# Expert weights loaded during the last attention slots into tiles that fall free there

## The chip, the cores and the metric

The kernel runs on one core of a Trainium2 chip. The metric is the device time of one execution in microseconds (us). A run of a kernel on one core counts as slow when it is over 1.5% above the fastest of the same kernel; verdicts use the other runs, called fast. Lnnn is a line of the kernel; lines of the changed kernel stand 9 to 30 higher than the same ones of the kernel before. In the views of the profile PE is TensorE (matrix products), DVE VectorE, ACT ScalarE, POOL GpSimd, and SPq the queue of transfers that SyncE issues. The clock is the share of TensorE's full clock that was granted; in the clock records it is either 1.00 or 0.50. An f32 product stands in the traces as two passes.

## The reference, cut to what matters

```python
# 1. DeltaNet attention: q, k, v of (4, 8, 768, 48), a recurrence over 768 tokens
y[:, :, t] = einsum('bhd,bhde->bhe', q[:, :, t], state)
v_old = einsum('bhde,bhd->bhe', state, k_n[:, :, t])
state = state + beta[t] * einsum('bhd,bhe->bhde', k_n[:, :, t], v[:, :, t] - v_old)
# 2. soft MoE: x (3072, 384), phi (384, 32), 8 experts of 4 slots
logits = x @ phi
d = softmax(logits, over tokens);   slot_input = d.T @ x          # 32 x 384
for e in range(8):
    slot_out[e] = relu(slot_input[e] @ w1[e]) @ w2[e]             # w1 384x1024, w2 1024x384
out = softmax(logits, over slots) @ slot_out                      # 3072 x 384
```

Everything is f32. One expert's first or second weights are 1536 KB (1.573 MB), all of them 25.2 MB. The experts need `slot_input`, which is complete only after the last token: whatever of the weights isn't in the core's memory by then is waited for.

## The kernel before

Attention runs in 24 slots, one for each chunk of 32 tokens. Four chunks make a group, and each group's routing (logits, running maximum, exponentials, the product for the experts' slots) is spread over the slots that follow. The last group's routing has nothing to be spread over and runs alone at the end. The parts that matter here:

```python
    for x in range(NCH):                      # 24 slots
        ...
        if 0 <= x + 4 < NCH:
            load_v(x + 4)
        if 8 <= x < 8 + NW1 * NKT:            # NW1 = 1: expert 0's first weights, in thirds
            load_w1((x - 8) // NKT, wpool, NW1, slice((x - 8) % NKT, (x - 8) % NKT + 1))
        ...
    for part in route(NG - 1, ...):           # the last group's routing, alone
        for name in ("head", "act", "mid", "vec", "end"):
            drain(part.get(name, []))
    att.close()                               # attention's memory becomes free

    wp2 = ctx.enter_context(tc.tile_pool(name="wts2", bufs=1, reuse_waits="tile"))
    for e in range(E):
        if e >= NW1:
            load_w1(e, wp2, 4)
        if e % 4 == 3:
            for i in range(e - 3, e + 1):
                load_w2(i, wp2, 6)
    ...                                       # slot inputs sl
    first(0); second(0); first(1); second(1)  # experts 0-3, then 4-7
    sj = wp2.tile([P, Dm], F32, name="sj")
    nc.vector.tensor_copy(sj, pso)            # what both second layers summed
    ...
    for i in range(24):                       # 24 output tiles of 192 KB (cut)
        nc.tensor.matmul(po, lhsT=cT..., rhs=so...)
        ob = wp2.tile([P, Dm], F32, name="ob", tag="ob", bufs=6)
        ...                                   # copy po to ob, on DVE or ACT by turns
        nc.sync.dma_start(out=out[...], in_=ob)
```

All these loads go through one queue, SyncE's, in the order of the built program: in the trace three first weights from 215.8 us, four second weights from 266.6, four first from 268.6, four second from 279.1. A tile in `wp2` lies over attention's dead tiles, and the program has its load wait until the last reader of what it covers is done: the last slots product ends at 266.5 us, and the first second weights go out at 266.61.

## Time and profile before

| | kernel before |
|---|---|
| median of 3 runs | 344.42 us (343.04 to 345.03) |
| span of the profiled run | 341.1 us |
| end of the last slots product (attention's end) | 266.5 us |
| last product of the experts, `sj` begins | 322.3 us |
| from `sj` to the end | 18.8 us |

The first part of the page, each engine's busy time with its share of the span and its instructions:

```profile
PE 276.1 (81%) x6887; PEld 215.8 (63%) x6887; DVE 220.2 (65%) x798; ACT 164.3 (48%) x341; POOL 161.2 (47%) x342
```

An 81% on PE looks like a kernel at its limit. It is an average of two kernels in a row, one short of TensorE and one short of bytes; the prediction takes them apart with the slices, the chain and the queue.

### The profile page before, as it was taken

The page shows a single profiled execution, that of the slowest core. Times are in us where ns is not written, and L with a number is a line of the kernel's source. Part 1 is how long each engine was busy: PE and PEld are TensorE (multiplying, and loading weights), DVE is VectorE, ACT ScalarE, POOL GpSimd, SP SyncE. Part 2 cuts the span into 40 slices and gives each one's busy share as a digit, 9 for nine tenths or more (in the row PEclk, how much of TensorE's full clock was granted, in tenths as well). Part 3 has the DMA queues.
Part 4 walks back from the last instruction along what each step waited for, and adds up shares of the span by engine and source line. Part 5 has one row for each costly group of instructions (what it writes and reads, how often), then busy time and mean ns, then how long its engine had stood idle before and what let it go on. Part 6 is the DMA issues. An engine that isn't in the chain of part 4 may idle for free.

```text
span 341.1 us, 16091 instructions
## 1 busy us (share of the span) xinstructions
PE 276.1 (81%) x6887; PEld 215.8 (63%) x6887; DVE 220.2 (65%) x798; ACT 164.3 (48%) x341; POOL 161.2 (47%) x342
## 2 busy tenths in 40 slices
PE   3885586888889997899989979899995887473884
PEld 3674485777768886788868868788874532020252
DVE  8399989766999897997999999942212210000043
ACT  3463155677758754777568545654752110010042
POOL 8976395648486597429970999932000000000000
PEclk9767659999999999999999995999998999998785
DMA  7855455554554455552012200600062699996078
GB/s 140 158 96 89 79 90 92 84 76 76 84 81 78 74 125 118 91 117 49 16 21 34 40 18 11 209 7 3 4 251 122 238 428 428 431 428 266 0 249 304
DMA packets 79766, 45.22 MB, mean 133 GB/s; under 512 B 73936, under 2 KB 77040, under 8 KB 77776
## 3 DMA queue, kind: packets, MB, share of 16 engines
q1 hardware_dynamic: 77904, 42.98, 45.8%
q0 software_dynamic: 704, 1.03, 1.6%
q8 instruction: 54, 0.88, 1.1%
q10 hardware_dynamic: 1088, 0.20, 0.3%
q14 instruction: 16, 0.13, 0.1%
HBM read 39.47 MB, written 4.72 MB: 130 GB/s over the span
## 4 chain that ended last, share of the span: by engine, by line
PE 46%; DVE 22%; DMA 13%; ACT 10%; issue 4%; SPq 2%; POOL 1%; DVEq 0%; POOLq 0%; ACTq 0%
DMA w2t<-in_moe_w_dram 12%; PE psR L445 7%; PE psS L458 6%; PE pt L596 5%; PE psY L475 4%; PE pt L238 4%; PE pso L891 4%; DVE prM L314 4%; PE psR L431 4%; PE pt L493 4%; ACT S L465 3%; PE pt L209 3%; DVE prE L314 3%; DVE nm L319 3%; DVE tt L319 2%
## 5 line engine op out<-in xcount | busy, mean ns | idle before, releaser
L395 POOL TENSOR_SCALAR V<-V,nT 128x48 f32<-128x48 f32 x192 | 90.8, 497 | 18.9 <-DMA V<-in_v_dram 9.7
L403 POOL TENSOR_SCALAR_AFFINE_SELECT Ab<-GQ 32x256 f32<-32x256 f32 x96 | 48.3, 503 | 12.2 <-PE psY L475 8.0
L465 ACT ACTIVATE S<-psS 48x768 f32<-48x768 f32 x46 | 37.1, 806 | 23.7 <-PE psS L458 23.4
L445 PE MATMUL psR<-R,Tb 64*64 64x48 f32 x768 | 29.7, 227 | 9.4 <-DVE R L438 6.7
L238 PE MATMUL pt<-KQ 48*32 48x64 f32 (+1 forms) x1792 | 25.7, 231 | 12.0 <-ACT KQ L225 6.8
L445 PEld LDWEIGHTS psR<-R,Tb 64*64 64x64 f32 x768 | 26.6, 141 | 13.2 <-issue 5.8
L238 PEld LDWEIGHTS pt<-KQ 48*32 48x32 f32 x1792 | 20.7, 115 | 18.3 <-ACT KQ L225 8.5
L319 DVE TENSOR_TENSOR nm<-nm,prM 128x16 f32<-128x16 f32 (+7 forms) x96 | 30.3, 316 | 0.0
L314 DVE TENSOR_TENSOR prM<-tt,lb 128x16 f32<-128x16 f32 (+7 forms) x96 | 30.1, 314 | 0.0
L475 PE MATMUL psY<-U,Ab 64*64 64x48 f32 x768 | 28.1, 224 | 0.1
L242 ACT ACTIVATE GQ<-pt 128x256 f32<-128x256 f32 (+1 forms) x56 | 16.7, 351 | 22.1 <-PE pt L238 21.5
L438 DVE TENSOR_TENSOR R<-V,psR 128x384 f32<-128x384 f32 x24 | 13.2, 550 | 21.1 <-PE psR L431 15.2
L475 PEld LDWEIGHTS psY<-U,Ab 64*64 64x64 f32 x768 | 25.1, 138 | 2.7 <-issue 0.7
L319 DVE TENSOR_TENSOR tt<-tt,prE 128x30 f32<-128x30 f32 (+7 forms) x90 | 25.6, 285 | 0.0
L458 PE MATMUL psS<-U,K 32*112 32x96 f32 x736 | 25.5, 278 | 0.0
L314 DVE TENSOR_TENSOR prE<-tt,lb 128x30 f32<-128x30 f32 (+7 forms) x90 | 25.3, 281 | 0.2 <-DVE nm L319 0.2
L448 ACT ACTIVATE U<-psR 128x384 f32<-128x384 f32 x24 | 11.8, 492 | 27.7 <-PE psR L445 22.7
L408 ACT ACTIVATE Tb<-TT,own 128x256 f32<-128x256 f32 x48 | 21.7, 504 | 6.1 <-DVE TT L386 6.1
L458 PEld LDWEIGHTS psS<-U,K 32*112 32x112 f32 x736 | 21.6, 183 | 4.1 <-issue 1.7
L431 PE MATMUL psR<-S,KQ 128*32 128x96 f32 x768 | 22.4, 258 | 1.2 <-ACT S L465 0.7
L431 PE MATMUL psY<-S,KQ 128*32 128x96 f32 x768 | 22.1, 256 | 1.2 <-issue 1.2
L891 PE MATMUL pso<-w2t,hT 128*32 128x384 f32 x128 | 16.0, 585 | 8.6 <-DMA w2t<-in_moe_w_dram 8.1
(143 smaller groups left out, 538.6 us busy)
## 6 DMA issues: line engine op xcount, KB each, us to landing
w2t<-in_moe_w_dram SPq DMA_DIRECT2D x8, 1536.0 KB, 18.8
w1t<-in_moe_w_dram SPq DMA_DIRECT2D x7, 1536.0 KB, 14.5
Q<-in_q_dram SPq DMA_DIRECT2D x96, 48.0 KB, 2.8
out_dram<-ob SPq DMA_DIRECT2D x24, 192.0 KB, 2.4
K<-in_k_dram SPq DMA_DIRECT2D x88, 48.0 KB, 2.6
V<-in_v_dram SPq DMA_DIRECT2D x80, 48.0 KB, 2.7
w1t<-in_moe_w_dram SPq DMA_DIRECT2D x3, 512.0 KB, 4.3
V<-in_v_dram POOLq DMA_DIRECT2D x16, 48.0 KB, 3.2
```

Of the source, the lines that this page charges most:

```text
L238: nc.tensor.matmul(pg[g][rh, b], lhsT=kq[r, b, 0, rh], rhs=kq[r, b, a0:a1, rh], start=True, stop=True, skip_group_check=True)
L314: nc.vector.tensor_tensor(pr, a.broadcast_to([P] + shape), b.broadcast_to([P] + shape), op=ALU.mult)
L319: nc.vector.tensor_tensor(dst, dst, pr, op=op)
L395: nc.gpsimd.tensor_scalar(Vt[cc][:, u], Vt[cc][:, u], nT[n][:, c * U + u:c * U + u + 1], None, op0=ALU.mult)
L403: nc.gpsimd.affine_select(out=Ab[cc % NT][r, :, h % 2, :].rearrange("p (b g) t -> p b g t", g=G), in_=GQ[n][r, c, :, :, 1, :], compare_op= ...
L408: nc.scalar.activation(Tb[cc % 2][:, :, x, :], TT[n][:, c * U:(c + 1) * U, :], ACT.Identity, scale=own[:, x:x + 1])
L431: nc.tensor.matmul(dst[hs[h], b].rearrange("p g d -> p (g d)"), lhsT=kq[:, b, a, hs[h]], rhs=old[:, h, b, :], start=(b == 0), stop=False, ...
L445: nc.tensor.matmul(pw[half[y], u], lhsT=T[y][:, u], rhs=st["R"][half[y], u], start=(u == 0), stop=True, skip_group_check=True)
L458: nc.tensor.matmul(psS[0:DP + D, h, b * GD:(b + 1) * GD], lhsT=K[hs[h], b * G:(b + 1) * G].rearrange("p g d -> p (g d)")[:, 0:DP + D], rhs ...
L465: nc.scalar.activation(new[r, :, :, g * D:(g + 1) * D], psS[r, :, 0:B * GD].rearrange("p h (b g e) -> p h b g e", b=B, g=G)[:, :, :, g], A ...
L475: nc.tensor.matmul(qs[half[y], b, g], lhsT=at[y][:, u], rhs=st["U"][half[y], u], start=False, stop=True, skip_group_check=True)
L891: nc.tensor.matmul(pso[C * j:C * j + C], lhsT=hT[q][:, t, C * j:C * j + C], rhs=w2t[4 * q + j][:, t, :], start=(q == 0 and t == 0), stop=( ...
```

## The change

Intent: issue first weights while the queue is nearly idle. Tiles that attention no longer needs in its last nine slots, such as a chunk's transposed keys and queries, are moved into a pool that outlives attention, and take 21 pieces of first weights (512 KB each). Second weights go into what is dead then and into tiles that the first layers set free.

```diff
+    lp = ctx.enter_context(tc.tile_pool(name="long", bufs=1))
...
-            KQ[cc] = wk.tile([P, B, 2, P], F32, name="KQ", tag="KQ", bufs=LEAD + 1)
+            KQ[cc] = lp.tile([P, B, 2, P], F32, name="KQ", tag="KQ", bufs=LEAD + 1)
...                      (GQ, tt, lb, TT and the Q tiles move to lp likewise)
+    free = {15: "GQ", 16: "KQ tt Q0 Q1", 17: "KQ", 18: "KQ", 19: "KQ TT GQ", 20: "KQ tt lb",
+            21: "KQ", 22: "KQ", 23: "KQ TT GQ"}
     for x in range(NCH):
...
+        preload(free.get(x, ""))     # one first-weight piece into each tile (two into a GQ)
...
-    for e in range(E):
-        if e >= NW1:
-            load_w1(e, wp2, 4)
-        if e % 4 == 3:
-            for i in range(e - 3, e + 1):
-                load_w2(i, wp2, 6)
+    for e in range(5):
+        load_w2(e, range(NFC), wp2.tile([P, NFC * Dm], F32, name="w2t", tag="w2t", bufs=5))
...
     first(0)
+    load_w2(5, range(NFC), wpool.tile([P, NFC * Dm], F32, name="w2t", tag="w0", bufs=1))
+    for t in range(0, NFC, 2):
+        load_w2(6, range(t, t + 2), room("KQ"))
+    load_w2(7, range(0, 5), room("GQ"))
+    load_w2(7, range(5, 7), room("KQ"))
+    load_w2(7, range(7, 8), room("tt"))
+    first(1)
     second(0)
-    first(1)
     second(1)
...
-            ob = wp2.tile([P, Dm], F32, name="ob", tag="ob", bufs=6)
+            ob = wp2.tile([P, Dm], F32, name="ob", tag="ob", bufs=10)
```

More of the change, by code (lines that the diff above doesn't have):

```diff
@@ L77 @@
     Ks = [io.tile([P, U, DP], F32, name=f"K{i}", bufs=1) for i in range(NK)]
-    Qs = [io.tile([P, U, DP], F32, name=f"Q{i}", bufs=1) for i in range(NQ)]
+    Qp = [lp.tile([P, 2, U, DP], F32, name=f"Q{i}", bufs=1) for i in range(NQ // 2)]
+    Qs = [Qp[i // 2][:, i % 2] for i in range(NQ)]
     Vt = {}
@@ L175, with room, load_w1, load_w2 @@
         nc.vector.memset(t, 0.0)
-    NW1 = 1
-    w1t, w2t = {}, {}
-    def load_w1(e, pool, bufs, parts=None):
-        if e not in w1t:
-            w1t[e] = pool.tile([P, NKT, F], F32, name="w1t", tag="w1t", bufs=bufs)
-        src = moe_w1[e].rearrange("(p k) f -> p k f", k=NKT)
-        if parts is None:
-            nc.sync.dma_start(out=w1t[e], in_=src)
-        else:
-            nc.sync.dma_start(out=w1t[e][:, parts], in_=src[:, parts])
-    def load_w2(e, pool, bufs):
-        w2t[e] = pool.tile([P, NFC, Dm], F32, name="w2t", tag="w2t", bufs=bufs)
-        nc.sync.dma_start(out=w2t[e], in_=moe_w2[e].rearrange("(p t) d -> p t d", t=NFC))
+    w1s = [[None] * NKT for _ in range(E)]
+    w2s = [[None] * NFC for _ in range(E)]
+    LONG = dict(KQ=([P, F], LEAD + 1), GQ=([P, 2 * F], 3), tt=([P, F], 2), lb=([P, F], 1),
+                TT=([P, F], 2))
+    def room(tag):
+        if tag in LONG:
+            shape, bufs = LONG[tag]
+            return lp.tile(shape, F32, name="w" + tag, tag=tag, bufs=bufs)
+        return Qp[int(tag[1])].rearrange("p a u d -> p (a u d)")
+    cells = [(e, k) for e in range(1, E) for k in range(NKT)]
+    def load_w1(e, ks, t):
+        nc.sync.dma_start(out=t[:, 0:len(ks) * F].rearrange("p (k f) -> p k f", f=F),
+                          in_=moe_w1[e].rearrange("(p k) f -> p k f", k=NKT)[:, ks[0]:ks[-1] + 1])
+        for i, k in enumerate(ks):
+            w1s[e][k] = t[:, i * F:(i + 1) * F]
+    def load_w2(e, ts, t):
+        nc.sync.dma_start(out=t[:, 0:len(ts) * Dm].rearrange("p (t d) -> p t d", d=Dm),
+                          in_=moe_w2[e].rearrange("(p t) d -> p t d", t=NFC)[:, ts[0]:ts[-1] + 1])
+        for i, j in enumerate(ts):
+            w2s[e][j] = t[:, i * Dm:(i + 1) * Dm]
+    def preload(tags):
+        for tag in tags.split():
+            t = room(tag)
+            for i in range(2 if tag == "GQ" else 1):
+                e, k = cells.pop(0)
+                load_w1(e, [k], t[:, i * F:(i + 1) * F])
     KQ, GQ, TT, nT = {}, {}, {}, {}
@@ L230, in products @@
             if n not in GQ:
-                GQ[n] = wk.tile([P, GC, B, G, 2, C], F32, name="GQ", tag="GQ", bufs=3)
+                GQ[n] = lp.tile([P, GC, B, G, 2, C], F32, name="GQ", tag="GQ", bufs=3)
             pg = [pt([P, B, na, C]) for _ in range(G)]
@@ L259, in unit @@
         def unit():
-            tt = st["tt"] = wk.tile([P, size], F32, name="tt", tag="tt", bufs=2)
+            tt = st["tt"] = lp.tile([P, size], F32, name="tt", tag="tt", bufs=2)
             nc.gpsimd.memset(tt, 0.0)
@@ L269, in spread @@
         def spread():
-            lb = st["lb"] = wk.tile([P, size], F32, name="lb", tag="lb", bufs=1)
+            lb = st["lb"] = lp.tile([P, size], F32, name="lb", tag="lb", bufs=1)
             nc.vector.transpose(
@@ L383, in back @@
             if n not in TT:
-                TT[n] = wk.tile([P, C, C], F32, name="TT", tag="TT")
+                TT[n] = lp.tile([P, C, C], F32, name="TT", tag="TT", bufs=2)
             r = slice(half * HC, (half + 1) * HC)
@@ L752 @@
             load_v(x + 4)
-        if 8 <= x < 8 + NW1 * NKT:
-            load_w1((x - 8) // NKT, wpool, NW1, slice((x - 8) % NKT, (x - 8) % NKT + 1))
+        if 8 <= x < 8 + NKT:
+            if x == 8:
+                w0 = wpool.tile([P, NKT * F], F32, name="w0", tag="w0", bufs=1)
+            load_w1(0, [x - 8], w0[:, (x - 8) * F:(x - 7) * F])
+        preload(free.get(x, ""))
         follow = plan(n + 2) if c == GC - 1 and n + 2 < NG else None
@@ L812 @@
     pp = ctx.enter_context(tc.tile_pool(name="pp", bufs=1, space=PSUM, reuse_waits="tile"))
-    for e in range(E):
-        if e >= NW1:
-            load_w1(e, wp2, 4)
-        if e % 4 == 3:
-            for i in range(e - 3, e + 1):
-                load_w2(i, wp2, 6)
+    assert not cells
+    for e in range(5):
+        load_w2(e, range(NFC), wp2.tile([P, NFC * Dm], F32, name="w2t", tag="w2t", bufs=5))
     def bank(tag, shape):
@@ L867, in product @@
                     nc.tensor.matmul(ph[C * j:C * j + C], lhsT=sl[:, k, :],
-                                     rhs=w1t[4 * q + j][:, k, f * HF:(f + 1) * HF],
+                                     rhs=w1s[4 * q + j][k][:, f * HF:(f + 1) * HF],
                                      start=(k == 0), stop=(k == NKT - 1), skip_group_check=True)
@@ L891, in second @@
                 nc.tensor.matmul(pso[C * j:C * j + C], lhsT=hT[q][:, t, C * j:C * j + C],
-                                 rhs=w2t[4 * q + j][:, t, :],
+                                 rhs=w2s[4 * q + j][t],
                                  start=(q == 0 and t == 0), stop=(q == 1 and t == NFC - 1),
```

## The prediction

> **What bounds the kernel now.** The first view is the page's table of 40 slices, each 341.1 / 40 = 8.5 us long.
>
> ```profile
> PE   3885586888889997899989979899995887473884
> DVE  8399989766999897997999999942212210000043
> PEclk9767659999999999999999995999998999998785
> GB/s 140 158 96 89 79 90 92 84 76 76 84 81 78 74 125 118 91 117 49 16 21 34 40 18 11 209 7 3 4 251 122 238 428 428 431 428 266 0 249 304
> ```
>
> Two kernels in a row. Counting slices from 0, up to slice 30 (about 265 us) the attention half runs, in 24 slots (chunks of 32 tokens): PE is full, DVE to slice 26, and from slice 18 to 28 the DMA engines move almost nothing. From slice 32 to 35 it is the other way round: the queue runs flat at 428 to 431 GB/s, DVE is at 0 or 1 and PE has holes. Then come the outputs. The second view is the chain of work that ended last, from 262 us on.
>
> ```profile
> 262.32 4.22 PE pt L596 x64
> ...
> 266.56 0.02 SPq L193
> ...
> 267.94 15.93 DMA w2t<-in_moe_w_dram
> ...
> 283.91 4.78 PE pso L891 x55
> ...
> 289.08 25.01 DMA w2t<-in_moe_w_dram
> ...
> 314.14 8.09 PE pso L891 x58
> ...
> 322.26 0.57 DVE sj L907
> ```
>
> L596 is the last product of attention, L193 the issue of second weights, L891 the second layer. Of the 55.7 us between 266.56 and 322.26, 15.93 + 25.01 = 40.9 are waits for weights. Why they come so late is in the queue's own order of time:
>
> ```profile
> 215.84 34.48 SPq L187 DMA_DIRECT2D w1t<-in_moe_w_dram  x3
> 266.61 1.94 SPq L193 DMA_DIRECT2D w2t<-in_moe_w_dram  x4
> 268.60 10.41 SPq L187 DMA_DIRECT2D w1t<-in_moe_w_dram  x4
> 279.06 10.41 SPq L193 DMA_DIRECT2D w2t<-in_moe_w_dram  x4
> ```
>
> Three first-weight tiles went out before attention ended. The other twelve (4 + 4 + 4, 1536 KB = 1.573 MB each, 18.9 MB) start at 266.6 and end at 314.1: 47.5 us. By rate: 18.9 MB / 430 GB/s = 43.9 us, and the last landing is 2.6 us past the pure stream (four tiles issued at 266.6 are all there at 283.9: 17.3 us against 4 x 3.66 = 14.6), so 46.5; 1 us stays unexplained. This stretch is bound by bytes, and only by the bytes that wait for attention's memory. The third view is the table by stretch, whose columns are stretch, length, then busy time of PE, PEld, DVE, ACT, POOL with counts, clock, DMA share and GB/s:
>
> ```profile
> 288.00:296.00 8.00, 4.34 (x19) 0.91 (x12) 0.00 (x0) 0.00 (x0) 0.00 (x0) 1.00 1.01 429
> 304.00:312.00 8.00, 3.68 (x17) 1.25 (x14) 1.44 (x2) 0.59 (x1) 0.00 (x0) 1.00 1.01 432
> 312.00:320.00 8.00, 5.86 (x40) 1.91 (x44) 0.00 (x0) 0.00 (x0) 0.00 (x0) 0.57 0.04 13
> 328.00:336.00 8.00, 7.53 (x24) 5.17 (x24) 3.91 (x8) 3.85 (x8) 0.00 (x0) 0.62 1.03 367
> ```
>
> DMA is full to 312. Then PE, which had starved, gets its last weights at 314.14 and runs at a clock of 0.57: its 58 products take 8.09 us where the same work at full clock took 4.78 (x55). The last line is the output stage: 367 GB/s of writes.
>
> [...] The loads here run at 428 to 432[...]. [...] here a first 1.573 MB tile lands after 6.2 us at the least, 2.5 us over its 3.66. [...] matmuls after the gap that ended at 314.14 (2.85 us, with only 2 matmuls in the 6.1 us before it) pace at 0.16 us, before and later at 0.08; single gaps of 1.7 to 2.8 us between 280 and 300 left the clock at 1.00.
>
> **The change part by part.** I built both kernels and compared instruction order and tile addresses. On POOL, DVE and ACT the order is the same; on PE it differs only after attention. Instruction counts don't change, nor do bytes (25.2 MB of weights). What moves is the time at which 21 pieces of first weights and some second weights start.
>
> 1. First weights, experts 1 to 7: 21 pieces of 512 KB (11.0 MB) go out in slots 15 to 23, each into a tile whose last reader is in an earlier slot. In the trace before, slots 15 to 23 are 183 to 252 us, nearly free of DMA; 11.0 MB at 430 is 25.6 us of 69. The last three pieces wait for the last chunk's weights (ACT at 249.6) and land by about 256. Nothing of it reaches the path: first layers start at 269.8 (as before).
>
> 2. Second weights: experts 0 to 4 lie in the pool opened after attention, over its dead tiles. In the built program, expert 0's tile lies over K tiles that are dead long before, and goes out right behind the last first weights (about 250, landing about 260), as does a quarter of expert 6. Expert 1's tile lies over the last `dr`, read until 266.54, and the queue is in order: so 1 to 4 start at 266.6, exactly like the first four of before, landed at 283.9. Behind them 2.75 tiles remain (5, three quarters of 6, 7). They wait for the first layer of experts 0 to 3, which ended at 277.7, while the queue is still busy to about 282; so there is no hole. 2.75 x 3.66 = 10.1 us: the last byte lands at 283.9 + 10.1 = 294.0, and expert 7's first five eighths 3/8 x 3.66 = 1.4 us earlier, at 292.6. Path before: 314.1. Saved on the stream: 20 us.
>
> 3. PE: first layer of 0 to 3 to 277.7, as before. In the built order the second half-layer follows with the turns woven in: 8 matmuls, 8 transposes (1.13 us), 40 matmuls at 0.1076 us (four in 0.43 us in the timeline, f32 products are two passes each): 278.7 + 1.2 + 4.3 = 284.2; mask, turns and copies of before took 304.9 to 307.2, i.e. 2.3, so 286.6. Second layer of 0 to 3: 64 passes x 0.081 = 5.2, four of them already done: 291.5. Second layer of 4 to 7 needs expert 7's first piece from its fourth product on: it stops at about 291.9 and goes on at 292.6, with 58 passes x 0.081 = 4.7: 297.3. [...] this costs 4.7 where before it cost 8.1. PE and DMA end almost level here: with all weights in place PE alone would end at 296.7.
>
> 4. The end: from the last product to the end of the span 341.1 - 322.3 = 18.8 us, mostly writes. The output tiles go from 6 to 10. In the chain the first outputs are spaced 0.50 us, by issue; later ones 0.54 us, by waiting for a free tile. At most 24 x 0.04 = 1 us is to be had; the DMA share of 1.03 says that the engines are nearly full anyway, so I take 0.4.
>
> Sum: last product 322.3 to 297.3, -25.0; outputs -0.4: span 341.1 to 315.7. The timed median is 344.42, so 344.4 - 25.4 = 319.0.
>
> **The rivals.** (a) *Nothing gained, as the bytes are the same.* If DMA bound the whole kernel, moving loads would not help. The GB/s row speaks against it: eleven slices with 3 to 49 GB/s apart from one. Time would stay at 344. (b) *The early loads slow attention.* They share the in-order queue with V, and in slots 16 to 19 a V load stands behind up to four pieces (2.1 MB, 4.9 us). V is loaded four slots ahead and first touched two slots later, some 16 us of slack at 8 us a slot; and the built waits name readers of the slot before. In the trace before, the 1.5 MB load at 215.8 and those at 250 went by without slots becoming longer. I grant 0 to 3 us. (c) *A tile frees later than meant and the queue stalls*, so that experts 4 to 7 land after 278 and PE waits for first weights. The margin is about 20 us; a full loss of step 1 would give some 15 us back (time about 334). (d) *PE as the new bound, cold.* [...] 64 passes at 0.16 cost 5 us more: 324. (e) *Smaller pieces move slower* (3 KB per partition and less in 2.36 MB)[...].
>
> **Range and chances.** Steps 2 and 3 rest on measured paces, and two independent limits meet within a microsecond, so a miss of one of them shows at once: (b), (d) and (e) all lengthen. On the short side, attention itself varies with the clock (the three runs of before spread 2 us), and outputs may gain the full 1 us. 315.5 to 323.5 holds it 8 times in 10. Faster by over 2% means under 337.5; only (a) or a full (c) with more on top prevents it: 0.97, 0.02, 0.01.
>
> **What would show it.** In the changed profile: DMA filled to some 150 to 200 GB/s in slices of 183 to 252 us; the last slots product as before at about 266.5 (if later than 269, rival b); no PE wait on first weights (else c); one run of about 430 GB/s from 267 to 294; a clock of 1.00 through the second layer (else d); the chain going from slots over transfers of `w2t` or the borrowed tiles to the last `pso` at about 297; from there 18.4 us to the end. The prediction is wrong if second weights other than experts 0 and part of 6 start before 266, or if the stream has a hole at 277 to 283 because the queue reaches expert 5's issue late.

## The result

The changed kernel took 326.0 us, median of 4 fast runs (322.73 to 327.15), beside 344.73 us for the kernel before in the same rounds. The ratio is 0.9445, with a 95% interval of 0.9365 to 0.9525: faster. (Ratios are the mean time of one kernel's fast runs over that of the other's of the same rounds, so not quite the ratio of the medians.) The time lies outside the predicted range of 315.5 to 323.5, on the long side. The profiled run is the longest of its four (span 325.4 us), whereas the profiled run of before lay 1.6 us under its median; this matters below.

The slices of the changed kernel, 8.1 us each:

```profile
PE   2896747888979999799998998796999958996890
PEclk9958559999999999679999999787899977999995
GB/s 132 164 100 90 69 91 94 70 88 89 81 79 82 78 83 129 93 82 130 50 13 26 144 175 220 91 87 259 202 69 66 221 218 112 432 422 341 4 308 273
```

From slice 22 (179 us) the DMA engines now move 66 to 259 GB/s beside attention, where in most slices they moved next to nothing before; the flat stretch at 422 to 432 GB/s has shrunk from four slices and a half to not quite three (34 to 36), and PE is full in the first two of them. In the clock row, slices 16, 17, 25 to 28, 32 and 33 show 6 to 8. The kernel before had only slices 24 and 30 under 9 between the start-up and its last layer.

The chain that ended last:

```profile
264.71 1.71 PE pt L597 x8
...
267.75 4.94 PE pt L615 x64
...
284.06 16.41 DMA wGQ<-in_moe_w_dram
300.52 5.36 PE pso L914 x58
305.90 0.57 DVE sj L937
```

It has the predicted shape: last slots product, first layers, one transfer, the 58 last passes. But the slots product ends at 272.7 and not at 266.5, expert 7's first piece (`wGQ`) lands at 300.5 and not at 292.6, and the 58 passes take 5.36 us and not 4.7. The queue, from the first early load on:

```profile
182.93 0.82 SPq L196 DMA_DIRECT2D wGQ<-in_moe_w_dram  x2
...
255.19 0.86 SPq L196 DMA_DIRECT2D wGQ<-in_moe_w_dram  x2
256.10 26.45 SPq L202 DMA_DIRECT2D w2t<-in_moe_w_dram  x6
...
284.06 0.43 SPq L202 DMA_DIRECT2D wGQ<-in_moe_w_dram  x1
```

All 21 pieces are issued by 256. Then the issues of expert 0 to 5 second weights stretch over 26.45 us: expert 0's goes out at once, at 256.1, expert 1's waits in front of everything behind it until attention's memory is free, and goes out at 272.7. So much had been read out of the built program. The stretch by stretch table (columns as in the prediction) around the end of the stream:

```profile
280.00:288.00 8.00, 7.97 (x74) 2.81 (x66) 1.44 (x2) 1.96 (x3) 0.00 (x0) 1.00 1.02 435
288.00:296.00 8.00, 7.66 (x84) 3.31 (x80) 1.44 (x2) 0.58 (x1) 0.00 (x0) 1.00 1.00 413
296.00:304.00 8.00, 5.01 (x58) 1.81 (x54) 0.00 (x0) 0.00 (x0) 0.00 (x0) 1.00 0.48 193
```

PE is full beside a full DMA, then has 3 us of holes in the last row, at a clock of 1.00. The view of waits names them: engine, line, what it waited for, us in total, times, longest.

```profile
PE pso L914 <- DMA wGQ<-in_moe_w_dram: 3.0, 1, 3.0
```

Laid beside the prediction's sum, for the profiled spans:

| stretch | predicted | measured | difference |
|---|---|---|---|
| start to the end of the last slots product | 266.54 | 272.69 | +6.15 |
| from there to expert 7's first piece landed | 26.1 | 27.83 | +1.7 |
| 58 passes of the second layer, to `sj` | 4.7 | 5.4 | +0.7 |
| `sj` to the end | 18.4 | 19.5 | +1.1 |
| span | 315.7 | 325.4 | +9.7 |

The medians miss by only 7.0 us: the profiled run of before lay 1.55 us under the median from which the prediction took its 25.4, and the profiled run of the change lies 1.15 us above its own.

### The profile page after: what moved, and what is told of

It is laid out like the page before. It is cut to its first block, busy times and chain, and to the rows that moved or that the text cites.

```text
span 325.4 us, 16112 instructions
## 1 busy us (share of the span) xinstructions
PE 269.7 (83%) x6887; PEld 217.0 (67%) x6887; DVE 219.7 (68%) x798; ACT 163.9 (50%) x341; POOL 160.5 (49%) x342
## 3 DMA queue, kind: packets, MB, share of 16 engines
q0 software_dynamic: 704, 1.03, 1.7%
## 4 chain that ended last, share of the span: by engine, by line
PE 50%; DVE 27%; DMA 8%; ACT 6%; issue 4%; SPq 3%; DVEq 0%; ACTq 0%
PE psR L464 6%; PE pt L615 6%; PE psS L477 6%; DMA wGQ<-in_moe_w_dram 5%; DVE prM L333 5%; PE psY L494 5%; PE psR L450 4%; PE pt L257 4%; PE pt L228 4%; DVE prE L333 4%; DVE nm L338 4%; PE pt L512 3%; DVE tt L338 3%; ACT S L484 2%; PE psY L450 2%
## 5 line engine op out<-in xcount | busy, mean ns | idle before, releaser
L422 POOL TENSOR_SCALAR_AFFINE_SELECT Ab<-GQ 32x256 f32<-32x256 f32 x96 | 48.0, 500 | 16.9 <-PE psY L494 12.7
L464 PE MATMUL psR<-R,Tb 64*64 64x48 f32 x768 | 29.0, 224 | 9.4 <-DVE R L457 6.4
L464 PEld LDWEIGHTS psR<-R,Tb 64*64 64x64 f32 x768 | 26.0, 139 | 13.0 <-issue 7.0
L257 PEld LDWEIGHTS pt<-KQ 48*32 48x32 f32 x1792 | 20.8, 116 | 18.7 <-ACT KQ L244 10.6
L338 DVE TENSOR_TENSOR nm<-nm,prM 128x16 f32<-128x16 f32 (+7 forms) x96 | 30.2, 314 | 0.0
L494 PE MATMUL psY<-U,Ab 64*64 64x48 f32 x768 | 29.7, 231 | 0.1
L494 PEld LDWEIGHTS psY<-U,Ab 64*64 64x64 f32 x768 | 26.6, 145 | 2.7 <-issue 0.8
L477 PE MATMUL psS<-U,K 32*112 32x96 f32 x736 | 26.4, 285 | 0.0
L477 PEld LDWEIGHTS psS<-U,K 32*112 32x112 f32 x736 | 22.4, 189 | 4.1 <-issue 1.7
L450 PE MATMUL psR<-S,KQ 128*32 128x96 f32 x768 | 23.2, 264 | 1.6 <-issue 0.9
L615 PE MATMUL pt<-Y,dr 64*64 64x97 f32 x384 | 21.6, 272 | 1.8 <-ACT dr L606 1.4
```

What stands on the lines that cost most here:

```text
L257: nc.tensor.matmul(pg[g][rh, b], lhsT=kq[r, b, 0, rh], rhs=kq[r, b, a0:a1, rh], start=True, stop=True, skip_group_check=True)
L338: nc.vector.tensor_tensor(dst, dst, pr, op=op)
L422: nc.gpsimd.affine_select(out=Ab[cc % NT][r, :, h % 2, :].rearrange("p (b g) t -> p b g t", g=G), in_=GQ[n][r, c, :, :, 1, :], compare_op= ...
L450: nc.tensor.matmul(dst[hs[h], b].rearrange("p g d -> p (g d)"), lhsT=kq[:, b, a, hs[h]], rhs=old[:, h, b, :], start=(b == 0), stop=False, ...
L464: nc.tensor.matmul(pw[half[y], u], lhsT=T[y][:, u], rhs=st["R"][half[y], u], start=(u == 0), stop=True, skip_group_check=True)
L477: nc.tensor.matmul(psS[0:DP + D, h, b * GD:(b + 1) * GD], lhsT=K[hs[h], b * G:(b + 1) * G].rearrange("p g d -> p (g d)")[:, 0:DP + D], rhs ...
```

## The experiments

My theory after the result: the bytes were taken off the path as predicted, and the largest miss, the later end of attention, is a matter of TensorE's clock at chance moments, not of the loads. The rival is the prediction's rival (b): the early loads lengthen the slots. Eleven runs were made, in three sets, each set on another chip and beside the kernel before (medians 344.41, 345.13 and 344.69 us); two of them repeat a kernel.

### Attention alone, with and without the early loads

In four kernels the expert layers are cut out, and the output stage takes a constant row. Their outputs are wrong, which doesn't matter for the times. Two come from the kernel before, two from the changed one (these with 6 output tiles, as before), each with and without loads.

```diff
 # short_after_none: the changed layout, no early loads
-    free = {15: "GQ", 16: "KQ tt Q0 Q1", ...}
+    free = {}
 # short_after_loads: all 21 pieces, expert 0's w2, a quarter of expert 6's; GpSimd reads one
 # column of each piece at the very end, so that none is dropped
+    nc.gpsimd.tensor_copy(junk[:, ...], w1s[e][k][:, 0:1])
 # all four: layers cut
-    first(0) ... second(1)
-    nc.vector.tensor_scalar(so, ps4, rd, None, op0=ALU.mult)
+    nc.vector.tensor_scalar(so, sacc[:, 0:1].broadcast_to([P, Dm]), rd, None, op0=ALU.mult)
```

> The kernel before with the expert layers cut out (the output stage multiplies by a constant row instead, so the result is wrong on purpose) and no expert weights but expert 0's first ones. It times attention plus the output stage alone, on the old layout, with nothing loaded late. Attention ended at 266.5 us in the profile before; about 3 us of set-up and 15.2 us of outputs follow, so about 286 to 288 us timed. This is the base of a two by two comparison: layout (old, new) and weight loads during attention (none, as in each kernel).

> The same with the three first-weight loads that the kernel before issues during the end of attention (1536 KB each). Theory 'chance' (attention's length differs between executions by spells of half clock, and loads do not matter): within 1.5 us of short_before_none. Theory 'loads slow attention': longer by an amount in proportion to 4.7 MB of 13, 1 to 2 us.

> The changed kernel cut in the same way, no weights loaded in slots 15 to 23. It tells the layout (tiles at other addresses) from the loads. Theories 'chance' and 'loads' both say within 1.5 us of short_before_none; a theory 'layout' (shared Q tiles, other addresses) says 2 us or more longer.

> The changed kernel cut in the same way, with all 21 first-weight pieces in slots 15 to 23 and expert 0's second weights behind them, as the changed kernel has them (each piece is touched once at the end by GpSimd so that its tile stays taken). Theory 'chance': within 1.5 us of short_after_none, and the profile shows half-clock spells at other places than the others, before slot 15 too. Theory 'loads slow attention', which is my rival b: 3 to 5 us longer than short_after_none, with the delay arising in slots 15 to 23.

| kernel | median us, fast runs | range | fast runs of 6 |
|---|---|---|---|
| short_before_none | 288.84 | 287.83 to 291.62 | 6 |
| short_before_loads (three late loads, as before) | 288.93 | 288.22 to 290.62 | 5 |
| short_after_none | 289.53 | 288.04 to 291.95 | 5 |
| short_after_loads | 290.95 | 289.43 to 292.95 | 5 |

The differences, 0.1 and 1.4 us for the loads and 0.7 and 2.0 us for the layout, are no larger than the scatter of each kernel over its own fast runs, some 2.4 to 3.9 us. As times, these runs leave room for either effect up to about 3 us. The two profiles of the changed layout say more, as both happened to have their clock spells in the same places. (Both were taken in runs that count as slow, 295.28 and 296.12 us, so they are compared only with each other.) TensorE's timeline in the last chunk, first without and then with the loads (start, us, engine, line, operation; a bracket gives idle time before it and what ended it):

```profile
256.70 1.14 PE L464 MATMUL psR<-R,Tb 64*64 64x48 f32 x32 [0.69 <-DVE sel L854]
...
261.50 1.55 PE L615 MATMUL pt<-Y,dr 64*64 64x97 f32 x32
```

```profile
256.72 1.14 PE L464 MATMUL psR<-R,Tb 64*64 64x48 f32 x32 [0.69 <-DVE sel L863]
...
262.15 0.38 PE L512 MATMUL pt<-ident,Y 128*96 128x128 f32 x2 [0.77 <-issue]
262.46 1.55 PE L615 MATMUL pt<-Y,dr 64*64 64x97 f32 x32
```

After 24 slots and 11 MB of loads beside them, the same product starts at 256.70 and 256.72 us. In this pair the loads did nothing to the slots. Only behind it does the kernel with loads lose 1 us, most of it in one pause of 0.77 us in which the profile shows nothing that TensorE waits for ("issue"). Whether its next instructions came late because of the stream is not shown, and nothing below rests on it. The same test over all thirteen profiles stands further down.

### Everything as in the change, but the first weights issued after attention

```diff
-        preload(free.get(x, ""))                     # in the slots
+    for x in sorted(free):                           # after attention
+        preload(free[x])
 # and in preload, a tiny GpSimd copy of attention's last result into each tile holds it back:
+            nc.gpsimd.tensor_copy(t[:, 0:1], sacc[:, 0:1])
```

> The changed kernel with the early loading undone: the 21 first-weight pieces go into the same tiles, but each tile gets a few numbers copied from attention's last result first, so that no piece can start before attention ends (the copies are overwritten by the load, the result stays right). The stream after attention is then 11.0 MB longer, 25.6 us at 430 GB/s. Stream: 23.2 MB, 54 us + 2.6 us after attention's end, then about 5 us of products and 19.5 us of outputs. Expected about 350 us (347 to 353), that is slower than the kernel before, which loads a quarter of that early; if the stream were not what the change shortens, it would stay near 326 us.

Correct, 352.03 us (349.96 to 354.9, 4 fast runs), ratio 1.0248 (1.0184 to 1.0312): slower than the kernel before, though whether by 2% stays unclear, as the interval includes it. Its chain:

```profile
270.60 8.32 DMA wKQ<-in_moe_w_dram
...
304.77 16.99 DMA wGQ<-in_moe_w_dram
321.81 7.05 PE pso L915 x58
```

The path after attention consists of transfers again, 62.0 us from the end of the slots product (266.9) to `sj`, against 33.2 in the changed kernel. The early start of the first weights is worth 29 us there and 26 us of the median. All of the change's gain comes from it: without it the kernel is 7 us slower than before, which had at least started three of these tiles (4.7 MB) ahead of attention's end. Its last layer also shows rival (d): after a pause of 4.2 us on TensorE the 58 passes take 7.05 us, not 5.36.

### The old order of the layers, and the old number of output tiles

```diff
 # layers_old
-    first(1)
     second(0)
+    first(1)
     second(1)
 # ob6
-            ob = wp2.tile([P, Dm], F32, name="ob", tag="ob", bufs=10)
+            ob = wp2.tile([P, Dm], F32, name="ob", tag="ob", bufs=6)
```

> The changed kernel with the layers in the old order: first and second layer of experts 0 to 3, then of 4 to 7. It tells what the second half of the change is worth. With it TensorE waits for second weights of experts 0 to 3 (the last landed 14 us after attention's end in the changed kernel, while their first layer is done 13 us after), then does the first layer of 4 to 7 (5 us) and its turns (2.3 us) while the stream runs; all is ready about 30 us after attention's end, the stream's last pieces at 28. Expected: same within 1.5 us; if the order matters, 2 to 4 us slower.

> The changed kernel with 6 output tiles instead of 10, as before. From the last second-layer product to the end the changed kernel took 19.5 us, before 18.8. Theory 'more tiles help the outputs' (my prediction, 0.4 us): 0.4 us longer. Theory 'writes are bound by the transfers, the tiles do not matter, or more in flight does harm': same within 0.5 us, or 0.6 us shorter, that is a stretch of 18.8 us in the profile.

layers_old is correct with 326.47 us (322.16 to 329.14), three of its six runs slow (the fast ones alone: 322.88); ratio of the fast ones 0.9382 (0.9329 to 0.9435). From the end of attention to `sj` it takes 32.5 us, where the changed kernel took 33.2 and, on its second run below, 32.5. The order of the layers is worth nothing that these few fast runs can show: either way the last layer stands waiting for expert 7 (3.0 us in the change, 2.0 here).

ob6 is correct with 325.66 us (323.45 to 327.22), ratio 0.9447 (0.9401 to 0.9494), so the time of the change itself (from attention's end to `sj` it took 34.8 us in its profile, so this stretch too differs by 1 to 2 us between profiles of the same program). Waits of DVE for an output tile, first with ten tiles (the change) and then with six, and the issue of the 24 outputs in the kernel before, the change and ob6:

```profile
DVE ob L951 <- DMA out_dram<-ob: 3.1, 6, 0.5
```

```profile
DVE ob L951 <- DMA out_dram<-ob: 5.6, 9, 1.5
```

```profile
325.95 12.14 SPq L924 DMA_DIRECT2D out_dram<-ob  x24
```

```profile
309.60 12.15 SPq L954 DMA_DIRECT2D out_dram<-ob  x24
```

```profile
309.09 12.16 SPq L954 DMA_DIRECT2D out_dram<-ob  x24
```

With more tiles DVE waits less, and the queue issues the 24 outputs in the same 12.15 us. What sets this pace is the transfers. In the packet records of all three runs an output has landed every 0.54 us from the first to the last (192 KB in 0.536 us are 367 GB/s), while the issues begin at a spacing of 0.50 us and fall back to 0.54 after about fourteen. Four more tiles gain nothing here. What remains of step 4 is that the span ends 3.65 us after the last issue in the change and in ob6, and 3.0 in the kernel before. This 0.65 us lies behind the outputs: from the last output packet to the end of the span it is 1.97 us in the change and in ob6, and 1.32 in the kernel before. In that time SyncE goes through ten semaphore instructions instead of five.

### A tile of its own for each of the five second weights

A tag names a set of buffers that tiles take by turns. In the built change, the five `w2t` buffers of one tag were laid out so that expert 1's tile covers what the last slots product reads. Expert 1's load stands second of them in the queue and goes out at 272.7 us, as attention ends. Experts 2 to 7 (but for a quarter of 6, issued at 253.9) follow it from 273.1 on, although much of what they cover is long dead. With tags of their own the tiles come in ascending order: experts 0 to 2 lie over tiles that die earlier, and only experts 3 and 4 have to wait.

```diff
-        load_w2(e, range(NFC), wp2.tile([P, NFC * Dm], F32, name="w2t", tag="w2t", bufs=5))
+        load_w2(e, range(NFC), wp2.tile([P, NFC * Dm], F32, name=f"w2t{e}", tag=f"w2t{e}", bufs=1))
```

> The changed kernel, but the five second-weight tiles of experts 0 to 4 get tags of their own, which puts them in ascending order over the dead attention tiles: experts 0 and 1 over K tiles, 2 over K, V and S, and only 3 and 4 over the tiles that are read until attention's end. So three tiles instead of one go out before attention ends. In the changed kernel TensorE stood 3.0 us waiting for expert 7's first piece. Theory 'the stream is still the last limit by 3 us, TensorE just behind': the wait goes, and the time falls by 2.5 to 3 us, to about 323. Theory 'my prediction's balance was right and the rest is attention': the wait would be under 1 us and nothing is gained.

Correct, 321.39 us (319.43 to 325.73, two of six runs slow; the fast ones alone 320.87), ratio 0.9311 (0.9267 to 0.9356). To rule out luck, it ran again beside the change itself:

> The changed kernel once more, unchanged, to see how far its attention half differs from run to run. If the attention half ends at a chance time set by half-clock spells (my theory), its profile may show the end of the last slots product anywhere from about 266 to 275 us (first profile: 272.7), and fast runs of 322 to 328 us. If the early loads lengthen it (rival), it is again at 272 or later. From there to the last layer's result 33 us, as before (33.2), whatever attention did.

> The version with a tag for each second-weight tile once more, beside the changed kernel on the same chip. If the gain of about 4.5 us is the stall before expert 7 and the late start of the stream, it repeats: 321 us, 3.5 to 5 us below the changed kernel of this call, and 29.4 us from the end of the last slots product to the last layer's result. If it was a lucky attention half, the two kernels lie within 1 us here.

after_again: 324.53 us (323.78 to 326.43, 6 fast runs), ratio 0.9452 (0.9404 to 0.95). own_again: 321.45 us (319.1 to 323.72, 6 fast runs), ratio 0.9356 (0.9295 to 0.9416). The gain repeats, as 3.1 us of the medians. Attention in after_again's profile ended at 270.2 and the rest took 32.5 us, both as the theory of chance has it (the rival wanted 272 or later). The gain of own_again was no lucky attention either: in these two profiles attention ends *later* with tags of their own (272.1 against 270.2). The gain is behind it, in own_again's chain:

```profile
278.01 5.28 PE ph L890 x46
...
291.00 10.49 PE pso L914 x124
```

No transfer is left in it. Both second layers run as one row of 124 products to 301.5, which is 29.4 us after attention's end, to the tenth what own_tags' first profile gave (268.7 to 298.2). The prediction had worked out that "with all weights in place PE alone would end at 296.7", which is 30.2 us after 266.54. That number was nearly right; the stream's was not, and the change was bound by the stream.

### TensorE kept busy through the last routing

The clock's part could be tested by itself. On top of own_tags, fifteen useless products of 128 by 128 go into the pauses of the last group's routing, into a tile of PSUM that is dead by then.

```diff
 # in route(), for the last group alone; t is lT or dT, which are in place at that point
+                    nc.tensor.matmul(psS[:, i % 4, 0:P], lhsT=ident, rhs=t, start=True, stop=True,
+                                     skip_group_check=True)
 # 3 before over_rows' turn, 1 behind by_tokens', 5 behind spread_max's, 6 behind repeat's
```

> As own_again, with 18 products of no use (128 by 128, into a dead tile) put into the pauses of the last routing, where TensorE rests, to keep its clock. Results stay right. If the half-clock spell at the end of attention (262 to 266 us at 0.50 in the earlier profile) comes from these pauses, the clock there is 1.00 (or at least 0.9), the four products before the slots take 1.1 instead of 2.1 us and the slots product 4.2 instead of 4.5, and the median is 1 to 2 us below own_again's. If spells come whatever TensorE does [...], the clock is as low as before and the time is the same or up to 1 us longer, for the added products.

The expectation says 18 products; there are 15, each of two passes in the trace. Correct, 318.33 us (315.86 to 321.26, one of six runs slow; the fast ones alone 317.80), ratio 0.9251 (0.9189 to 0.9312), 3.1 us below own_again in the median, where 1 to 2 were expected. The end of the routing in own_again, in TensorE's timeline and in a row of the table by stretch:

```profile
264.38 2.08 PE L597 MATMUL pt<-ident,dT 128*128 128x128 f32 x8 [1.09 <-ACT dT L587]
267.81 4.28 PE L615 MATMUL pt<-Y,dr 64*64 64x97 f32 x64 [1.36 <-ACT dr L606]
```

```profile
266.00:270.00 4.00, 2.64 (x31) 2.35 (x31) 0.00 (x0) 1.26 (x2) 0.00 (x0) 0.50 1.00 427
```

And the same two views of warm_end, where L608 and L627 are these two lines and L524 is the added product:

```profile
261.73 1.16 PE L608 MATMUL pt<-ident,dT 128*128 128x128 f32 x8
262.72 1.50 PE L524 MATMUL psS<-dT,ident 128*128 128x128 f32 x12
264.24 2.88 PE L627 MATMUL pt<-Y,dr 64*64 64x97 f32 x64
```

```profile
262.00:266.00 4.00, 3.98 (x62) 3.79 (x63) 0.20 (x2) 1.26 (x2) 0.00 (x0) 1.00 1.01 430
```

The same eight passes of L597 (L608) take 1.16 instead of 2.08 us, the same 64 of the slots product 2.88 instead of 4.28, at a clock of 1.00 instead of 0.50; for the slots product 4.2 had been expected. In own_again the clock falls at 263.9 us, after a pause of 0.81 us and in the middle of one of 1.09. From the end of the last logits to the end of the slots product it is 8.7 us instead of 10.5. That much, 1.8 us, comes from the clock in the routing's pauses: no other of the thirteen profiles has this stretch under 9.5 us. The means of the fast runs differ by 3.6 us (321.42 and 317.80), with an error of about 0.9 from the scatter of the runs; the rest may be scatter, and isn't explained here. From attention's end to `sj` it takes 29.4 us once more (267.1 to 296.5).

### All profiles side by side

Each run left one profile, so attention's end can be compared over thirteen. "Cold" is the time lost to a low clock, worked out from the table by stretch in steps of 4 us: the sum of 2 x (1 - clock) x 4, that is the us spent at half clock. The start-up is left out: there it is 10 to 31 us, and yet the second chunk begins its `psR` product within 57.2 to 58.8 us in all thirteen. The early loads begin at about 183 us. (The kernel before and short_before_loads have three loads from 216 us on; short_after_none and short_after_loads are slow runs.)

| profile | early loads | cold, 60 to 180 us | cold, 180 us to the last logits | last logits end | from there to the slots product's end | attention's end |
|---|---|---|---|---|---|---|
| before | no | 0.0 | 10.2 | 257.0 | 9.5 | 266.5 |
| late | no | 0.0 | 10.2 | 256.1 | 10.7 | 266.9 |
| short_before_loads | no | 0.0 | 10.2 | 258.1 | 10.7 | 268.8 |
| short_before_none | no | 0.0 | 13.6 | 259.4 | 11.7 | 271.1 |
| short_after_none | no | 10.2 | 17.0 | 264.1 | 10.7 | 274.8 |
| layers_old | yes | 0.0 | 6.9 | 258.4 | 10.7 | 269.1 |
| own_tags | yes | 0.0 | 13.7 | 258.0 | 10.7 | 268.7 |
| ob6 | yes | 0.0 | 13.6 | 259.0 | 11.7 | 270.6 |
| warm_end | yes | 3.4 | 10.2 | 258.4 | 8.7 | 267.1 |
| after_again | yes | 10.2 | 3.4 | 259.5 | 10.7 | 270.2 |
| own_again | yes | 12.7 | 6.9 | 261.6 | 10.5 | 272.1 |
| after | yes | 10.2 | 13.7 | 261.9 | 10.7 | 272.7 |
| short_after_loads | yes | 10.2 | 17.1 | 265.0 | 10.4 | 275.4 |

Add the two cold columns and the last logits follow them to within 1 to 2 us, loads or no loads: 256 to 258.4 at 7 to 10 us, 258 to 259.5 at 13 to 14, 262 at 20 to 24, 264 to 265 at 27. At 13.6 to 13.7 the kernels with loads are at 258.0 to 259.5 and the one without at 259.4. Nor do the loads make more cold time: beside them it is 3.4 to 17.1 us from 180 on (mean 10.7), without them 10.2 to 17.0 (mean 12.2). And the profile of before is the shortest of all thirteen, with a shorter tail than any but warm_end, which was made to be warm.

The slots themselves say the same. From chunk 15's `psR` product (L445, L464) to chunk 23's, which is the time of the early loads, it is 64.0 us in the kernel before and 66.9 in the change; over the five profiles without early loads 64.0 to 67.5 (mean 66.1), over the eight with them 64.5 to 67.5 (mean 66.6). The kernel before is again the shortest.

Nor do the cold spells come out of nothing. In TensorE's timelines each of the 25 spells at half clock that begin between 60 and 250 us has, in the 3.4 us before it, at least part of a pause of 1.4 to 2.9 us (in one case two pauses, of 1.15 and 0.64). The 3.4 us are the length of the shortest of these spells (one from 94.3 us in warm_end, one from 215.0 in after_again); the others last 6.8 to 6.9 or 10.2. The pauses stand before a `psR` product, which mostly waits for DVE's tile `R` (before three of the four spells in the profiles of before and the change; before the fourth, at 132.0 us in the change, the profile shows nothing that is waited for). A pause of 1.5 to 2.0 us there, at 92 to 94 us, is in all thirteen profiles, long before any early load; the clock falls after it in five of them. So the pauses are the program's own; what decides whether the clock falls after one isn't shown. All five are among the ten profiles of the changed layout and none among the three of the old one, but by chip they are as unevenly spread (none of the four profiles of the second set, all three of the third), so that this is too few to tell whether layout or chip has a part in it.

## Why the prediction was right or wrong

**Right: what bound the kernel, and which way the change goes.** Bytes that begin only after attention were the path; late, which differs from the change in the time of these loads alone (and some tiny copies), shows it with 26 us. The queue did not stall (rival c): the first layers ran without a wait for first weights. The clock stayed at 1.00 through the stream's end (rival d did not come). The gain in the median was 18.7 us instead of 25.4.

**Wrong, the largest term: attention's end.** The step "like the first four of before", from 266.6 on, and the check "the last slots product as before at about 266.5 (if later than 269, rival b)" took one profile's end as a constant. It came at 272.7, and 6.15 us follow from that. They split in the table above into 4.9 us up to the last logits and 1.25 in the tail. Of the 4.9, 2.0 are there before the early loads can act (chunk 15's `psR` product starts at 187.7 us instead of 185.7), and 2.9 arise in slots 15 to 23. Over this part the change's profile has 13.7 us more of cold time than that of before, and 10.2 of those lie before the first early load. In the tail, the kernel before happened to do L578 at full clock (its timeline; the change took 1.69 and 4.91 us for the same two):

```profile
259.81 1.16 PE L578 MATMUL pt<-ident,dT 128*128 128x128 f32 x8 [1.09 <-ACT dT L568]
262.32 4.19 PE L596 MATMUL pt<-Y,dr 64*64 64x97 f32 x64 [1.35 <-ACT dr L587]
```

The slots product's 4.2 us were themselves mostly cold, which the pace could have told: its 64 passes took 2 x 1.5 us inside the slots, and take 2.88 in warm_end. Nor did the trace of before give a length of pause after which the clock falls: single gaps of 1.7 to 2.8 us between 280 and 300 us left it at 1.00, but at 203.6 us, inside the slots, it fell after a single pause of 2.33 us. And the check could not tell its culprit: kernels without early loads, too, end attention anywhere from 266.5 to 274.8. Rival (b) is not what made the 6.15 us: the slots of the pair without and with loads coincide within 0.02 us, and cold time accounts for the ends with loads and without them alike. A large part of this miss is the choice of the sample: the profiled run of before lay low among its runs and that of the change high.

It is not all luck, though. An estimate for a run of average time: add to each profile's attention end what its run lacks to the mean of its kernel's fast runs, taking all that follows attention as constant. That gives 267.5 to 268.6 us for the three kernels of the old layout, 269.2 and 269.4 for the changed layout without early loads (late, short_after_none), and 269.4 to 271.0 for the seven runs with them (warm_end left out). So 2 to 3 of the 6 us stay when the luck of the two profiles is taken out, about 1 of them with the layout and 1 with the loads, each no larger than the scatter within the groups. Rival (b) had been granted 0 to 3 us; an effect of 1 to 2 us stays open.

**Off in size: the stream.** It needed 27.8 us after attention's end where step 2 had 26.1. Three things make the 1.7 us, and a little more. 0.3 are the first landing (6.5 us after its issue instead of 6.2). About 1.5 us fall between experts 3 and 4, whose tiles are complete at 286.6 and 291.8 us, 5.2 apart instead of 3.66. The completion of a tile is counted in sixteen steps (the page counts 16 DMA engines): up to 286.6 all sixteen come within 0.9 us, and from then on fifteen do and the last one comes 1.5 us after them, down to expert 7's first piece (298.98 and 300.48). In the packet records an instruction fetch of 16 KB, 1.07 us long, falls there, at 288.9 us, and a weight packet right behind it takes 0.93 us instead of 0.46, which together make the 1.5. The records don't name the engine, and no run removes the fetch, so that it is the cause is likely but not shown. The kernel before has such a fetch in its stream, too (0.96 us, at 287.7), and there, too, one step comes late from the next tile on, by 1.0 us (313.12 and 314.10 for the last tile): that is the "1 us" that "stays unexplained" in the prediction. The smaller pieces cost about 0.2 us (packets of 3,072 B move at 25.4 GB/s an engine, those of 12,288 B at 26.7), so rival (e) was right in its direction. "PE and DMA end almost level here" was therefore wrong: the gap, 0.7 us in the prediction (291.9 to 292.6), measured 3.0 us. own_tags removes this wait and gains 3 to 4.5 us.

**Off in size: the last layer**, 5.4 instead of 4.7 us. 58 x 0.081 leaves out the last pass itself, 0.49 us long, and the pace is nearer 0.085. That the clock would stay high over the gap before it was the estimate; the row of 296 to 304 us shows it at 1.00. The trace of before could have told the rest: there the second layer of experts 0 to 3 runs its 58 last passes at full clock, from 283.91 to 289.26 us, which is 5.35 us.

**Wrong in sign: the outputs.** "I take 0.4" for ten tiles; ob6 shows nothing gained, since the transfers set the pace (0.54 us for an output with six tiles and with ten), and a further 0.65 us went to SyncE's closing semaphore instructions. The prediction had read the 0.54 us as a wait for a free tile, where the tile was waiting for its transfer; its own line, a DMA share of 1.03 at 367 GB/s, said so.

The range was too narrow because its largest term was taken from one profile, and nothing in one profile says how far the next may lie from it. The thirteen profiles, with a spread of 266.5 to 275.4 for that term alone, do.

## What to carry to other kernels

Look for bytes that wait for memory rather than for data, and give them tiles that die earlier: 11 MB moved beside a busy TensorE, and the slots beside them took 66.6 us instead of 66.1 (means of eight and of five profiles). Then read the built placement of the tiles: in the change one early tile over a late reader, expert 1's, went out at 272.7 us, 16.6 us after the one before it, and held up all that stood behind it in the queue; a line that changed only tags gained another 3 to 4.5 us. Where TensorE runs in short bursts, take no stage's end from a single profile, and try idle products in the pauses, which took 1.8 us off the last routing here: with both, the tags and the idle products, the kernel ran at 318.3 us, below both kernels.
